# A new order of steps for a fused S5-scan and Hedgehog-attention kernel on one Trainium2 core

## The chip, the cores and the metric

The kernel runs on one core of one Trainium2 chip. The metric is the device time of one execution in microseconds (us), first instruction to last write. A core has a matrix engine (PE; its weight loads are listed apart as PEld), a vector engine (DVE), an activation engine (ACT), a general-purpose engine (POOL), and queues for DMA transfers, of which SP's is used most. Each engine works through its own list of instructions in order. Semaphores are the only tie between the lists.

## The reference

`x` has 2048 rows of 512. Two branches read it and a gate mixes them:

```python
x = A_x
g = _sigmoid((x * gate_w).sum(-1, keepdims=True))
a = _A_ref(x, ...)     # S5: h = Lam_bar * h + x @ B_bar over 2048 steps, y = 2 Re(h C) + x * Dskip
b = _B_ref(x, ...)     # q, k, v of 32 heads of 16; phi = [softmax(p), softmax(-p)]
return g * a + (1 - g) * b
...
# in _B_ref
kv = jnp.einsum("bhsf,bhsd->bhfd", phi_k, v)
num = jnp.einsum("bhqf,bhfd->bhqd", phi_q, kv)
den = jnp.einsum("bhqf,bhf->bhq", phi_q, z)[..., None] + 1e-6
o = num / den                                    # then o @ wo
```

## The kernel before

Rows are taken in 16 tiles of 128; row 8c + r is cell c of residue r. The scan is cut into eight residues, each step between residues being a matmul with a 128x128 block matrix of the powers of `Lam_bar` (`dg`), and a short scan over 64 groups of cells on DVE.

There is no loop nest to speak of. Every piece of work is a Python generator ("step") that issues a few instructions each time it is advanced. A table of some 1,300 tokens, `ORDER`, says in which order the generators are advanced; `k3@1` advances step `k3` and gives it PSUM bank 1, and `:D` puts that piece's copy or scaling on DVE instead of ACT. Since each engine runs its list in order, the table fixes the lists of all five engines:

```python
    for tok in ORDER.split():
        tok, _, banks = tok.partition("@")
        tok, _, eng = tok.partition(":")
        sel["eng"] = "dve" if eng == "D" else "act"
        sel["banks"] = [int(b) for b in banks]
        next(st[tok])
```

The PSUM banks are handed over by the same table: a step that is given bank 7 waits until the last reader of bank 7 is through.

The steps that matter here, by stage (`n` a tile, `m` one of eight blocks of states):

- **Start.** `Lk`, `Lx`, `Lv`, `Lb`, `Lc`, `Lq` load weights and `x` (transposing DMAs on SP's queue, L244 for `xT`); `Z` are matmuls on zeros that keep PE busy; `W`, `T`, `f` transpose and fold weights.
- **Small parameters.** `P`, `U`, `M` form `Lam_bar` and its powers on DVE in tiles of 128x8 (`dgs`; `M` has three parts, each squares the one before). `M2` carries on from the last of them on POOL: `M2`'s first part squares twice more (L419 to L421, twice), its second negates (L437), its third (L439 to L447, nine instructions) ends in two copies into `csp`, the scale factors of `C`. `dc` (L451, L452) stands on POOL between the second and the third.
- **Keys and queries.** `k`, `q`, `v` project a tile (L521) and copy it out of PSUM; for `q`, DVE also reads one column, `nge` (L555), and only then is the bank free. `x`, `n`, `e`, `s` (capital letters for queries) are the softmax pieces: maximum and minimum trees (L569), differences (L580, L587), exponentials on ACT (L594), sums and division. `a` adds up `kv`.
- **Scan.** `b` and `g` (L655, L660, L672 to L690) do the input products and the steps between residues; `z`, `sa`, `sb`, `H` the scan over groups and its corrections, which DVE adds into `HH` (L750).
- **C.** `c0` to `c3` scale the transposed `C` by `csp`, three parts each, into `CS` and `CT` (L470 on ACT, L472 on DVE); `C` and `A` move the results.
- **Fill-in of the other residues.** `hk`, `hd`, `ek`, `dk`: two scalings and two additions (L820, L822) per pair of blocks into `LS`.
- **Output.** `y` (L876, L883), `o` (L893; then L898, L901 on ACT and L907 on DVE), `O` (transposing DMA), `t` (L932, then a scaled copy out of PSUM), `R` the store.

The third part of `M2` ends so, and `c1`'s first part is the second line of `st_c`, with `j` = 1:

```python
        nc.gpsimd.tensor_copy(out=csp[0:HS], in_=dgb[0:HS, :, 0::2])
        nc.gpsimd.tensor_copy(out=csp[HS:P], in_=dgb[HS:P, :, 1::2])
...
    def st_c(j):
        scaled(CS[:, 1, j], CT[:, 0, j], csp[:, 1, j:j + 1])
```

Of the kernel before, what the change touches and what calls it, by code (L numbers as in the profile page):

```python
# [23 lines left out]
ORDER = """
Lk Z@0 Lk Z Z Z Z B Z B Z Z Z Z Z Lx Lx Z Z Z Z W00@2 Lx W01@1 W00 W01 W00 W01 W10@3 W11@4 W11:D f1@2 f0@1 T0@5 W10
f1 f0 T0:D Lx f2@4 V@3 T1@2 f3@6 Lx V f2 Z k0@5 P T1:D U P f3 k1@2 k1 Lv P2 P k0 P2 U k3@1 P2 k2@6 P2 k7@4 P2 P4 P3
P2 P3 P4 U Lx P4 i i M i Lb x0z U k5@0 k4@3 k1 M k3 k0 V2@1 i k7 i v0@4 n0 k5 x0 M k2 Lb v1@6 x0 n0 V2 k6@2 Lx v6@1
k4 i v3@3 k8@5 n0 x0 n0 x1 k9@0 n1 x0 Lx x1 L x0 n1 k10@7 n0 k6 v1 x2 M2 M2 Lx Lb x2 v6 e0 k11@2 x1 n1 x2 Lb k8 n1
x1 x2 x1 Da k13@5 v3 v0 Lq n2 k12@4 k15@3 k14@1 n1 dc n2 e1 s0 k9 k11 n2 x2 n2 b10@0 Da k15 k14 n2 Lc k10 s0 b10 k13
k12 g10@3 b00@2 M2 b31@5 b01@0 Lc s0 b21@4 x3 b20@7 e2 Lq Da s0 b11@1 e2 b00 x3 Db b30@6 g00@2 g10 b31 b21 w1@4 x3  # L30
g11@5 b01 Lc b20 g10 x4 s1 n3 g20@3 w1 w3@7 s1 s0 x4 b11 g20 gw g00 b30 Lc c1:D w2@6 c2 w3 g30@1 s1 g11 n3 w0@7 Da
s1 x3 g21@4 s0 g20 g31@3 Lb g00 g11 g21 s2 c0:D g30 c2 w0 g31 c2 s2 x4 g21 n3 Db x3 n4 w2 g21 n3 g11 g30 x4 g01@7
g21 g01 g11 s2 s1 g01 g21 g31 g11 g01 q3@1 g01 n4 g11 s2 g31 s1 g31 c3:D v4@6 c3 c1:D s0 n4 g31 g01 g31 g21 n3 q3 s2
x4 g31 g21 q0@2 g01 s2 Db s1 Lb g31 n4 g21 v4 q3 g11 q10@0 g01 g11 g21 q4@6 q0 e3 s2 v2@4 q0 n4 g11 g01 g31 c3:D g01
v5@1 q4 q2@3 z0@5 c0:D z0 q1@2 b61@7 z0 c1:D e3 q4 z0 s3 v2 a0@65 a0 q1 q10 b50@4 z0 s3 v5 q1 a1 q10 a1 a2 q7@1 s3
q2 a2 b40@0 e4 q7 N0 z0@2 q2 X0 g50@3 b61 a2 v7@7 z0 N0 X0 z0 X0 b50 q5@2 e4 C N0 v7 X0 b71@4 N0 q6@7 q7 c0 z0 X0 s3
q5 a2 s4 b40 A g50 N0 v9@1 q6 q5 X1 C q9@0 sa0@2 A b71 b60@4 g50 q6 v9 g40@1 X1 E0 N1 q9 C A g40 s4 b70@7 X1 b60 sa0
q8@2 X1 sb0@4 E0 s4 q9 N1 g70@3 b70 q8 X1 sb0 g40 s4 v8@0 g60@7 v8 s3 g70 s4 S0 H1@4 N1 S0 Lo g70 q8 g60 s3 G0 S0 N1
S0 v11@0 g71@2 b51@3 N1 g60 S0 g71 q11@1 H0@7 g71 S0 v11 g61@0 S0 C b51 s4 g61 H1 S0 v10@4 q11 g51@3 XX0 s3 a3 H0 E1
g71 v10 E1 g71 g71 g61 g51 b41@4 g51 g61 b41 XX0 A Ld a3 s4 a3 g61 g71 g51 g61 q11 a3 hd0 S1 X2 g41@1 g41 hd0 N2 g41  # L40
S0 g51 q13@4 g41 X2 g41 N2 X2 S1 g61 g71 g61:D g71 S0 G0 g51 XX0 S1 g51 g41 g41 v13@7 N2 g71 g51 S1 XX0 g51 hd0 g61
N2 X2 hd1 g41 g41 hd1 q12@2 g61 g41 g51 z1@1 v13 z1 z1 q14@0 v12@3 S1 hd0 q13 G0 z1 hd0 z1 z1@1 S1 hd1 v12 v15@7 z1
z1 q13 v14@1 z1 hd1 Ld X2 hd1 sa1@3 a4 v15 q15@4 sa1 v14 a4 N2 sb1@1 a4 sb1 END a4 Y hd0 Y q12 y0@3 H2@1 H3@7 S1 q14
Y E2 XX1 q14 Y H2 q15 y0 hk4 o3@5 o2@0 o2 H3 o3 o2 S1 XX1 q12 y3@7 y1@2 o3 y0 q15 E2 XX1 XX1 S1 o2 o0@0 o3 hd1 o0
o1@4 G1 y2@6 N3 y3 y2 o1 y1 y1 o0 hk6 o1 y3 S2 O1 hk4 o0 S2 o1 y2 O0 S1 N3 X3 hk6 o4@4 o5@0 hk6 hk4 hk6 o4 o4 hk4 S2
hk4 S2 t2 o4 hk6 o5 t2 hk4 S2 o5 t3 y4@5 t3 S2 y6@6 S2 ek0 o5 hk6 ek0 t0 X3 ek2 y5@7 S2 t0 y5 ek2 G1 O2 o7@3 X3 N3
ek2 X3 N3 ek0 o6@0 o6 y4 X3 o7 o6 t1 N3 o7 o6 S2 y5 S2 t5 ek0 o7 y7@0 ek0 y6 t1 y4 E3 o8@3 o9@1 ek2:D ek2 E3 ek0 ek4
o8 G1 y6 o8 y7 y7 ek2 ek4:D t4 o9 ek4 o9 ek6 O3 ek6:D ek6 t7 R1 t6 ek4:D ek6:D S3 o8 y9@3 y8@4 ek4 t6 o9 o10@1 ek4
t4 t5 t7 ek6 S3 y10@5 o10 ek6 o11@6 o10 XX2 XX2 y9 S3 y11@0 o11 y8 o10 O4 S3 R0 o11 y8 o11 S3 S3 y9 S3 y10 dk2 u10
S3 y11 dk0 S3 dk2:D t8 dk0:D dk0 dk0 dk2 R3 dk0 t9 dk2 O5 dk0 dk4 dk2 t10 dk4:D dk4 dk2 dk4:D y14@6 t8 dk4 t10 t11  # L50
t9 S3 dk6:D o12@4 o13@1 S3 dk6 o12 R4 y13@3 y12@7 o12 dk6:D o13 dk4 o13 o12 o14@4 o13 dk6 o14 R2 o14 dk6 dk6 y15@12
o14 y13 y12 o15@4 u11 y12 o15 y14 t11 o15 y14 y13 O6 t12 O7 R5 t13 t14 o15 O8 t12:D t13:D t14:D y15 R6 R7 y15 t15
t15 R8 t15 t15:D R8
"""
# [964 lines left out]
```

## Time and profile before

| | us |
|---|---|
| median of 3 executions | 146.94 (146.64 to 147.11) |
| the profiled execution, its whole time | 146.70 |
| its span, first to last instruction | 144.7 |
| PE, DVE, ACT, POOL busy in the span | 138.2, 132.9, 125.4, 21.9 |
| mean granted PE clock | 0.996 |

The profiled execution's time is 2.0 us above its span, and 0.24 us below the median. In the tables of the profile a row of the timeline gives start, length, engine, line of the kernel, operation, output and inputs, shape, and how many instructions were merged into it; lengths of neighbours overlap by some hundredths of a us to 0.17 us, since engines overlap the end of one instruction with the start of the next, so what an instruction adds to a full engine is the distance from its start to the next one's. PE has 986 matmuls and the trace holds records of 971 of them; a hole of exactly one matmul's length on PE is a missing record and no wait.

### The profile page before, as it was taken

The page shows a single profiled execution, that of the slowest core. Times are in us where ns is not written, and L with a number is a line of the kernel's source. Part 1 is how long each engine was busy: PE and PEld are TensorE (multiplying, and loading weights), DVE is VectorE, ACT ScalarE, POOL GpSimd, SP SyncE. Part 2 cuts the span into 40 slices and gives each one's busy share as a digit, 9 for nine tenths or more (in the row PEclk, how much of TensorE's full clock was granted, in tenths as well). Part 3 has the DMA queues.
Part 4 walks back from the last instruction along what each step waited for, and adds up shares of the span by engine and source line. Part 5 has one row for each costly group of instructions (what it writes and reads, how often), then busy time and mean ns, then how long its engine had stood idle before and what let it go on. Part 6 is the DMA issues. An engine that isn't in the chain of part 4 may idle for free.

```text
span 144.7 us, 2815 instructions
## 1 busy us (share of the span) xinstructions
PE 138.2 (96%) x971; PEld 74.9 (52%) x986; DVE 132.9 (92%) x313; ACT 125.4 (87%) x245; POOL 21.9 (15%) x40
## 2 busy tenths in 40 slices
PE   6999999999999999999999999999999999999990
...
DVE  5389999999999999999999999999999999999560
ACT  0899998999999999999999999999999996984110
...
GB/s 115 219 231 230 202 184 201 174 212 131 5 70 2 0 128 239 0 67 107 181 64 210 211 89 116 146 173 150 202 112 127 273 189 243 210 290 163 117 137 36
DMA packets 55957, 21.56 MB, mean 149 GB/s; under 512 B 44552, under 2 KB 55944, under 8 KB 55944
## 3 DMA queue, kind: packets, MB, share of 16 engines
...
q8 instruction: 7, 0.11, 0.4%
q14 instruction: 6, 0.05, 0.1%
...
## 4 chain that ended last, share of the span: by engine, by line
PE 79%; DMA 9%; SPq 4%; DVE 3%; issue 1%; ACT 1%; ACTq 0%
PE PS L521 20%; PE PS L876 17%; PE PS L660 10%; PE PS L655 10%; PE PS L932 9%; DMA xT<-in_A_x_dram 7%; PE PS L645 3%; SPq L244 3%; PE PS L893 2%; DMA CS<-in_B_wqkv_dram 2%; PE PS L672 2%; PE PS L883 2%; DVE HH L750 1%; PE PS L678 1%; SPq L249 1%
## 5 line engine op out<-in xcount | busy, mean ns | idle before, releaser
L594 ACT ACTIVATE EE<-EE 128x2048 bf16<-128x2048 bf16 x16 | 31.8, 2002 | 0.5 <-DVE EE L587 0.5
L521 PE MATMUL PS<-WKV,xT 128*128 128x480 bf16 (+1 forms) x124 | 28.8, 373 | 0.4 <-DMA xT<-in_A_x_dram 0.2
L521 PEld LDWEIGHTS <-xT 128*128 128x128 bf16 x192 | 18.3, 99 | 19.1 <-DMA xT<-in_A_x_dram 0.6
L876 PE MATMUL PS<-C,LS 128*128 128x512 bf16 (+1 forms) x102 | 22.7, 362 | 0.1
L141 ACT CAST Xq<-PS 128x480 bf16<-128x480 f32 x32 | 19.0, 640 | 0.2
L655 PE MATMUL PS<-xT,BT 128*128 128x512 bf16 x64 | 16.1, 379 | 0.0
L141 ACT CAST LS<-PS 128x512 bf16<-128x512 f32 x24 | 15.8, 735 | 0.1
L521 PE MATMUL PS<-Wq,xT 128*128 128x481 bf16 x64 | 15.6, 368 | 0.0
L660 PE MATMUL PS<-xT,BT 128*128 128x512 bf16 x64 | 15.5, 379 | 0.0
L932 PE MATMUL PS<-Wo,oT 128*128 128x512 bf16 (+2 forms) x64 | 14.8, 366 | 0.2
L569 DVE TENSOR_TENSOR EE<-EE 128x256 bf16<-128x256 bf16 (+3 forms) x54 | 14.6, 302 | 0.0
L876 PEld LDWEIGHTS <-LS 128*128 128x128 bf16 x104 | 9.3, 98 | 9.3 <-DVE LS L822 0.3
L938 ACT ACTIVATE ot<-PS,G 128x512 bf16<-128x512 f32 (+1 forms) x11 | 7.0, 671 | 5.4 <-PE PS L932 5.3
L907 DVE TENSOR_TENSOR on<-PS,rd 128x512 bf16<-128x512 f32 x16 | 10.6, 680 | 0.5 <-ACT rd L901 0.4
L470 ACT ACTIVATE CT<-HH,dgs 128x512 bf16<-128x512 bf16 x16 | 11.1, 722 | 0.0
L569 DVE TENSOR_TENSOR EE<-Xq 128x1024 bf16<-128x1024 bf16 (+1 forms) x18 | 11.0, 623 | 0.0
L141 ACT CAST vx<-PS 128x512 bf16<-128x512 f32 x16 | 10.9, 710 | 0.0
L470 ACT ACTIVATE CT<-CS,nsn 128x512 bf16<-128x512 bf16 x15 | 10.6, 726 | 0.0
L580 DVE TENSOR_TENSOR EE<-Xq,EE 128x2048 bf16<-128x2048 bf16 (+1 forms) x9 | 10.0, 1110 | 0.0
L587 DVE TENSOR_TENSOR EE<-EE,Xq 128x2048 bf16<-128x2048 bf16 (+1 forms) x9 | 9.9, 1105 | 0.0
L660 PEld LDWEIGHTS <-BT 128*128 128x128 bf16 x64 | 6.1, 98 | 6.9 <-issue 0.2
L932 PEld LDWEIGHTS <-oT 128*128 128x128 bf16 x68 | 6.2, 98 | 6.6 <-DMA oT<-on 0.7
...
## 6 DMA issues: line engine op xcount, KB each, us to landing
...
```

The lines of the kernel that those rows point to most:

```text
L141: nc.scalar.copy(out=out_ap, in_=in_ap)
L470: nc.scalar.mul(out=out_ap, in_=in_ap, mul=s_)
L521: MM(out=pt[:], lhsT=xT[:, kt, ti * P:(ti + 1) * P], rhs=W[:, kt, 0:pt.shape[-1]], start=(kt == 0), stop=(kt == KT - 1))
L569: VT(out=dst, in0=cur[:, :, :, 0:n, :], in1=cur[:, :, :, n:2 * n, :], op=op)
L580: VT(out=half(EE, 0), in0=X5, in1=live["mx", p].to_broadcast([P, L, 8, Dh, 4]), op=ALU.subtract)
L587: VT(out=t, in0=live["mn", p].to_broadcast([P, L, 8, Dh, 4]), in1=X5, op=ALU.subtract)
L594: aexp(out=EE[:, l_:l_ + w], in_=EE[:, l_:l_ + w], func=ACT.Exp)
L655: MM(out=pt[:], lhsT=BT[:, m, kt, :], rhs=cells(kt, r), start=(kt == 0), stop=False, skip_group_check=True)
L660: MM(out=pb[:], lhsT=BT[:, m, kt, :], rhs=cells(kt, 2 * pr), start=(kt == 0), stop=(kt == KT - 1))
L876: MM(out=py[:], lhsT=hs[m], rhs=C2[:, m, c:c + w], start=(m == 0), stop=False)
L907: VT(out=live["on", g_][:, u], in0=pn[:, :, :, 0:Dh], in1=rd[:].unsqueeze(3).to_broadcast([P, 2, 16, Dh]), op=ALU.mult)
L932: MM(out=py[:], lhsT=oT[:, g, :], rhs=Wo[:, g, c:c + w], start=False, stop=(g == HG - 1))
```

## The change

Only the table `ORDER` is different; every generator, buffer, shape and DMA is the same, and each token is still there as often as before. So the engines get the same work in another order, except that some of the `:D` marks moved: nine pieces go from DVE to ACT (`T0`, `c0`'s first part, one evacuation of `g61`, four scalings of `dk`, the copies of `t12` and `t14`) and seven from ACT to DVE (`f0`, `c3`'s second part, one scaling of `ek6`, four of `dk`). Banks are given out anew too.

```diff
 ORDER = """
...
-k4 i v3@3 k8@5 n0 x0 n0 x1 k9@0 n1 x0 Lx x1 L x0 n1 k10@7 n0 k6 v1 x2 M2 M2 Lx Lb x2 v6 e0 k11@2 x1 n1 x2 Lb k8 n1
-x1 x2 x1 Da k13@5 v3 v0 Lq n2 k12@4 k15@3 k14@1 n1 dc n2 e1 s0 k9 k11 n2 x2 n2 b10@0 Da k15 k14 n2 Lc k10 s0 b10 k13
-k12 g10@3 b00@2 M2 b31@5 b01@0 Lc s0 b21@4 x3 b20@7 e2 Lq Da s0 b11@1 e2 b00 x3 Db b30@6 g00@2 g10 b31 b21 w1@4 x3
...
+n1 k12@4 U k13@0 Lq M U k14@2 x2 s0 x1 s0 n1 s0 k8 k15@5 v1 x2 g00@6 M2 M2 k11 dc M2 x2 k10 n2 e1 b00@7 k13 Da b10@0
+k12 Lc k15 b11@1 b20@5 k14 n2 b21@4 v3 x3 c1:D s0 x4 n3 Lc Lq Db b00 Da Db e2 x3 e2 x4 b21 g11@7 g20@3 b30@2 s1 b20
...
```

Three places of the lists are used by the prediction, all on DVE. In an order row, `128x32x64` is the 128x2048 of the profile, `128x16x64` its 128x1024.

**The last squaring of `M` on DVE.** `ssm_par` and `dgs` are the tiles of the powers; POOL's `M2` waits for the row `L421` of the last of the three parts. Before, that part stands between the first trees of the keys:

```order
L569 TENSOR_TENSOR EE<-Xq 128x16x32 x2
L419 TENSOR_TENSOR ssm_par<-dgs 128x32
L420 TENSOR_TENSOR dgs<-ssm_par 128x8
L421 TENSOR_TENSOR dgs<-ssm_par 128x8
L569 TENSOR_TENSOR EE<-EE 128x16x16 x2
L356 CAST vecm<-PS 128x8
```

Now:

```order
L366 RECIPROCAL ssm_par<-ssm_par 128x8
L419 TENSOR_TENSOR ssm_par<-dgs 128x32
L420 TENSOR_TENSOR dgs<-ssm_par 128x8
L421 TENSOR_TENSOR dgs<-ssm_par 128x8
L368 TENSOR_SCALAR ssm_par<-ssm_par 128x8
L569 TENSOR_TENSOR EE<-EE 128x32x8
L569 TENSOR_TENSOR smk<-EE 128x1024
L580 TENSOR_TENSOR EE<-Xq,EE 128x16x64
L569 TENSOR_TENSOR smk<-smk 128x32x16
L587 TENSOR_TENSOR EE<-EE,Xq 128x16x64
```

It moved back, behind the first two groups of keys, to just ahead of the first row of sums, `smk<-EE`.

**The first use of `csp` on DVE**, `c1`'s first part (L472, `CS<-CT,csp`). Before:

```order
L569 TENSOR_TENSOR EE<-Xq 128x32x32
L569 TENSOR_TENSOR smk<-smk 128x32x16
L569 TENSOR_TENSOR EE<-EE 128x32x16
L415 CAST Wq_85<-vecm 128x4
L472 TENSOR_SCALAR CS<-CT,csp 128x512
L569 TENSOR_TENSOR smk<-smk 128x32x8
```

Now, a little further down the same list as the rows of the first place:

```order
L569 TENSOR_TENSOR smk<-smk 128x32x8
L569 TENSOR_TENSOR EE<-EE 128x32x4
L580 TENSOR_TENSOR EE<-Xq,EE 128x32x64
L569 TENSOR_TENSOR EE<-EE 128x32x4
L458 CAST dgv<-dgs 64x3x2x8x4
L460 CAST dgv<-dgs 64x24x4 x2
L587 TENSOR_TENSOR EE<-EE,Xq 128x32x64
L569 TENSOR_TENSOR EE<-Xq 128x32x32
L472 TENSOR_SCALAR CS<-CT,csp 128x512
L569 TENSOR_TENSOR smf<-smk 128x128
```

It moved forward, to two rows behind the first `L587 ... 128x32x64`; POOL's own list is the same but for one exchange ahead of `M2`.

**The hand-over from the scan to the output on DVE.** `L750 HH<-PS,HH 128x2x256` are the last additions of the scan, `L555 nge` frees a bank of a query, `L629` is a long product of the query features, `L907` an output tile. Before, with the second `L847` and what follows:

```order
L555 TENSOR_SCALAR nge<-PS 128x1
L847 SCALAR_TENSOR_TENSOR KVm<-PS,eps_p,maskN 128x16
L750 TENSOR_TENSOR HH<-PS,HH 128x2x256 x2
L629 TENSOR_TENSOR EE<-EE,rho 128x32x64
L555 TENSOR_SCALAR nge<-PS 128x1 x2
L907 TENSOR_TENSOR on<-PS,rd 128x512 x2
```

Now:

```order
L847 SCALAR_TENSOR_TENSOR KVm<-PS,eps_p,maskN 128x16
L750 TENSOR_TENSOR HH<-PS,HH 128x2x256 x2
L555 TENSOR_SCALAR nge<-PS 128x1 x2
L629 TENSOR_TENSOR EE<-EE,rho 128x32x64
L555 TENSOR_SCALAR nge<-PS 128x1
L907 TENSOR_TENSOR on<-PS,rd 128x512 x2
```

Two of the three `nge` reads stand ahead of the long `L629` now instead of one; with the new banks (`y1@5`, `y2@4`, `y3@2` in place of `y3@7`, `y1@2`, `y2@6`) the first two output tiles behind `o3` and `o2` take the banks that these two free.

More of the change, by code (lines that the diff above doesn't have):

```diff
@@ L24 @@
 ORDER = """
-Lk Z@0 Lk Z Z Z Z B Z B Z Z Z Z Z Lx Lx Z Z Z Z W00@2 Lx W01@1 W00 W01 W00 W01 W10@3 W11@4 W11:D f1@2 f0@1 T0@5 W10
-f1 f0 T0:D Lx f2@4 V@3 T1@2 f3@6 Lx V f2 Z k0@5 P T1:D U P f3 k1@2 k1 Lv P2 P k0 P2 U k3@1 P2 k2@6 P2 k7@4 P2 P4 P3
-P2 P3 P4 U Lx P4 i i M i Lb x0z U k5@0 k4@3 k1 M k3 k0 V2@1 i k7 i v0@4 n0 k5 x0 M k2 Lb v1@6 x0 n0 V2 k6@2 Lx v6@1
-k4 i v3@3 k8@5 n0 x0 n0 x1 k9@0 n1 x0 Lx x1 L x0 n1 k10@7 n0 k6 v1 x2 M2 M2 Lx Lb x2 v6 e0 k11@2 x1 n1 x2 Lb k8 n1
-x1 x2 x1 Da k13@5 v3 v0 Lq n2 k12@4 k15@3 k14@1 n1 dc n2 e1 s0 k9 k11 n2 x2 n2 b10@0 Da k15 k14 n2 Lc k10 s0 b10 k13
@@ L30 @@
-k12 g10@3 b00@2 M2 b31@5 b01@0 Lc s0 b21@4 x3 b20@7 e2 Lq Da s0 b11@1 e2 b00 x3 Db b30@6 g00@2 g10 b31 b21 w1@4 x3
[L31 to L53, printed above, removed]
+Lk Z@0 Z Z B Z Z Lk Lx Lx Z Lx Z Z Z Z Z Z Z Z Lx Z Lv W01@1 Z W00@2 W00 B W01 W00 W10@3 W11@4 Lx W01 f1@2 f0@1 T0@5
+V@0 W10 W11:D f0:D T1@3 Lb f3@6 f1 f2@4 V T1:D T0 P P P2 k0@5 f3 P2 Lx f2 P2 k1@2 k2@6 P2 P P2 k0 Lb P4 P4 k1 Lx
@@ new lines @@
+k3@1 P4 P3 P2 i k0 U i k1 i V2@4 n0 x0 P3 k4@3 i Lx k5@0 k6@2 n0 M k2 U k4 V2 k3 x0 k5 i x1 k6 x0 k7@4 n0 v6@1 x0
+v3@3 i n1 v1@6 M v0@2 k7 n1 n0 x1 L x0 n0 x2 k9@0 Lx v6 e0 x0z n2 k8@5 x1 Lb Lc n2 x2 n1 Lb n2 x1 k11@1 v0 k10@7 k9
+n1 k12@4 U k13@0 Lq M U k14@2 x2 s0 x1 s0 n1 s0 k8 k15@5 v1 x2 g00@6 M2 M2 k11 dc M2 x2 k10 n2 e1 b00@7 k13 Da b10@0
+k12 Lc k15 b11@1 b20@5 k14 n2 b21@4 v3 x3 c1:D s0 x4 n3 Lc Lq Db b00 Da Db e2 x3 e2 x4 b21 g11@7 g20@3 b30@2 s1 b20
+g00 x3 x4 g21@4 b10 g20 s1 c0 b30 b11 g10@0 n4 w3@1 s1 x3 c1:D n3 Lc g00 g20 g10 n4 s1 w0@6 b31@5 c2 g10 s0 s0 g11
@@ new lines @@
+n4 w0 g21 x4 g30@0 s2 b01@6 Da s2 g30 w2@3 b31 c2 gw c2 b01 g30 g11 Da g31@5 g11 x4 g31 g21 w3 n3 g21 w1@6 s2 g01@0
+s0 w1 c3:D s2 g01 s1 g01 g21 g11 w2 g31 q3@1 s2 Lb n4 g01 n3 x3 g21 g11 g01 s1 g31 g21 q3 v4@6 g01 g11 g21 g31 q0@2
+Db v4 c0:D n3 c3:D v2@6 g31 g11 g11 e3 s2 Lb q3 s1 g01 g01 g31 g21 g31 v5@1 c1:D q2@3 n4 g21 g01 g31 g11 c3:D q0
+b61@7 g01 g31 s2 q10@0 z0@5 q0 Ld z0 e3 b50@4 q10 q4@2 z0 s3 q2 v2 q10 q1@5 z0 a0@60 a0 v5 q4 s3 a1 a1 v7@1 z0 a2 q1
+e4 v7 s3 q4 q2 z0@2 q9@3 N0 q1 q5@5 e4 X0 a2 q7@1 z0 C b61 z0 a2 N0 q5 Ld z0 X0 s3 X0 v9@2 b50 N0 s4 q6@7 X0 b40@4
@@ new lines @@
+s4 a2 q9 v9 q7 q9 b70@3 q6 q5 Lo c0 v8@5 N0 g70@2 X0 q6 C N0 b70 s3 X1 N1 b40 E0 X1 C C g50@3 sa0@4 g50 A b71@7 q7
+s4 X1 g70 sa0 E0 g40@1 b71 X1 b60@4 g40 v8 b60 s4 g60@7 X1 S0 q8@4 sb0@5 N1 G0 S0 N1 g50 S0 v11@3 g70 sb0 A s3 g60
+g71@2 g71 H1@5 s4 A g40 v10@1 q8 g60 N1 S0 S0 b51@7 g71 N1 v11 S0 XX0 H1 s4 S0 E1 g51@3 b41@5 b51 g71 v10 g51 S0 A
+XX0 H0@7 s3 hd1 g51 g71 b41 g51 g71 g41@1 H0 a3 q11@7 g51 g41 E1 g41 g71 s4 g61@5 g51 g61 q11 g41 S1 g61 hd0 g71 g51
+g61 a3 g51 a3 hd0 q8 g41 a3 S1 q11 g61 g61 q13@4 G0 S1 g41 g61 X2 g71 g41 hd1 S0 hd0 g71 g51 N2 v13@7 g61 g61 g41
@@ new lines @@
+g41 S1 X2 g51 g41 XX0 S0 N2 q12@2 g61 hd1 q13 XX0 z1@1 q14@5 S1 v13 v12@3 X2 N2 z1 z1 N2 z1 G0 z1 q13 hd0 hd0 S1
+z1@1 v12 hd1 v15@7 q12 v14@3 z1 z1 v15 X2 z1 sa1@1 hd1 X2 a4 a4 q15@4 sa1 sb1@1 v14 a4 N2 a4 q15 sb1 XX1 XX1 y0@3 S1
+q14 Y H2@1 H3@7 Y y0 E2 Y y0 Y H2 H3 o3@0 hk4 END o2@6 XX1 q14 q15 y1@5 o3 S1 o2 XX1 o2 q12 o3 y2@4 o2 o0@6 S1 y3@2
+E2 o3 o1@0 hk6 hd0 o0 y3 y2 X3 y1 o1 hd1 y2 y3 o0 y1 S2 o0 o1 O1 o1 hk4 hk4 hk4 hk6 N3 S2 o5@0 hk6 o4@6 o4 O0 hk4 t2
+S2 o5 o4 hk4 S2 o4 ek0 S2 o5 N3 S1 S2 o5 t2 t3 y5@7 X3 y4@6 S2 hk6 t3 ek0 t0 t1 y7@0 S2 ek0 X3 o7@1 hk6 t0 N3 O2 t1
```

7 lines of the change are left out of this document (added).

## The prediction

> **What bounds the kernel now.** I read the page's shares and slices first, then DVE and PE in stretches, then POOL and DVE row by row where the lists change, then the waits of the tail.
>
> ```profile
> span 144.7 us, 2815 instructions
> PE 138.2 (96%) x971; PEld 74.9 (52%) x986; DVE 132.9 (92%) x313; ACT 125.4 (87%) x245; POOL 21.9 (15%) x40
> PE   6999999999999999999999999999999999999990
> DVE  5389999999999999999999999999999999999560
> ACT  0899998999999999999999999999999996984110
> ```
>
> Three engines are full at once until about 130 us. PE ends last, but DVE runs beside it without air:
>
> ```profile
> 27.50:80.00 52.50, 52.24 (x351) 27.29 (x355) 52.37 (x108) 52.27 (x97) 5.52 (x7) 1.00 0.59 102
> 80.00:90.00 10.00, 9.83 (x71) 5.29 (x69) 9.69 (x27) 9.70 (x28) 4.36 (x4) 1.00 0.71 141
> 90.00:133.00 43.00, 42.29 (x352) 23.24 (x357) 42.61 (x85) 39.79 (x82) 0.46 (x1) 1.00 0.92 188
> ```
>
> The columns are the stretch and the busy time of PE, PEld, DVE, ACT, POOL. From 27.5 to 133 us DVE idles 0.13 + 0.31 + 0.39 = 0.83 us in all. What ties it to PE at the end:
>
> ```profile
> 132.35 0.69 DVE L822 TENSOR_TENSOR LS<-CT 128x1024 bf16<-128x1024 bf16 x1
> PEld L876 <- DVE LS L822: 0.3, 1, 0.3
> ```
>
> The last addition of `dk6` ends at 133.04, and PE's weight load for the `y` that reads it waits 0.3 us; PE's margin there is some 0.07 us (the matmuls start at 133.11), and 7.8 us of PE work follow. So DVE's list up to this row is a second critical path, as long as PE's. PE cannot end earlier by more than this row does, and any delay on DVE from 27.5 us on that its 0.83 us of idle time doesn't take up comes out at the end.
>
> **The change, part by part.** *DVE's list up to `dk6`.* Ahead of that row six scalings (0.26 us each) and `f0` (0.34) came in, and five scalings, `T0` (0.41) and a small copy (0.14) went out: about +0.05 us, as an estimate from the rows' start-to-start times. So the order alone brings DVE there no sooner; only waits can differ.
>
> *A new wait: `c1` on POOL.* POOL's `M2` and `dc`, first and last rows and the third part in full:
>
> ```profile
> 15.49 0.24 POOL L419 TENSOR_TENSOR ssm_par<-dgs 128x32 f32<-128x32 f32 x1
> ...
> 17.67 0.69 POOL L437 TENSOR_SCALAR nsn<-dgs 128x16 f32<-128x16 f32 x1
> 22.31 0.11 POOL L452 MEMSET decay<- 128x8 f32 x1 [3.94 <-ACT decay L451]
> 22.38 0.46 POOL L439 TENSOR_TENSOR ssm_par<-dgs,vec 128x32 f32<-128x32 f32 x1
> 22.91 0.26 POOL L440 TENSOR_TENSOR dgb<-ssm_par 128x8 f32<-128x8 f32 x1
> 23.14 0.64 POOL L441 TENSOR_TENSOR dgb<-ssm_par 128x8 f32<-128x8 f32 x1
> 23.86 1.28 POOL L442 TENSOR_TENSOR dgb<-dgb,vec 128x16 f32<-128x16 f32 x1
> 25.22 0.69 POOL L443 TENSOR_TENSOR dgb<-dgb,ssm_par 128x16 f32<-128x16 f32 x1
> 26.02 1.41 POOL L444 TENSOR_SCALAR dgb<-dgb,sgn 128x8 f32<-128x8 f32 x1
> 27.39 0.34 POOL L445 TENSOR_SCALAR dgb<-dgb 128x8 f32<-128x8 f32 x1
> 27.80 0.50 POOL L446 COPY csp<-dgb 64x12 f32<-64x12 f32 x1
> 28.34 0.56 POOL L447 COPY csp<-dgb 64x12 f32<-64x12 f32 x1
> ```
>
> `csp` is ready at 28.90. DVE in the same stretch:
>
> ```profile
> 14.16 0.16 DVE L421 TENSOR_TENSOR dgs<-ssm_par 128x8 f32<-128x8 f32 x1
> ...
> 20.05 0.69 DVE L580 TENSOR_TENSOR EE<-Xq,EE 128x1024 bf16<-128x1024 bf16 x1
> 20.65 0.34 DVE L458 CAST dgv<-dgs 64x192 bf16<-64x192 f32 x1
> ...
> 22.04 0.68 DVE L587 TENSOR_TENSOR EE<-EE,Xq 128x1024 bf16<-128x1024 bf16 x1
> ...
> 23.04 0.68 DVE L569 TENSOR_TENSOR smk<-EE 128x1024 bf16<-128x1024 bf16 x1
> ...
> 23.86 1.21 DVE L580 TENSOR_TENSOR EE<-Xq,EE 128x2048 bf16<-128x2048 bf16 x1
> ...
> 25.15 0.68 DVE L463 TENSOR_TENSOR dg<-I,dgv 128x1024 bf16<-128x1024 bf16 x1
> 25.75 1.24 DVE L587 TENSOR_TENSOR EE<-EE,Xq 128x2048 bf16<-128x2048 bf16 x1
> ...
> 27.57 0.69 DVE L569 TENSOR_TENSOR EE<-Xq 128x1024 bf16<-128x1024 bf16 x1
> ...
> 32.61 0.35 DVE L472 TENSOR_SCALAR CS<-CT,csp 128x512 bf16<-128x512 bf16 x1
> ```
>
> Before, `c1` comes at 32.61, 3.7 us behind `csp`. Now it stands two rows behind the `L587` of 25.75, whose own place hardly moves: ahead of it `f0` and two rows of sums (0.34 + 0.41 + 0.21) came in, and `T0` and one `L463` (0.41 + 0.60) went out, so -0.05 us. 25.70 + 1.16 + 0.60 (start to next start of that row and of the 27.57 row) puts DVE before `c1` at 27.5.
>
> POOL starts later at the same time. The rows between the last squaring of `M` and that `L587` add up, start to start (0.60 for a 128x1024, 1.14 for the long L580, 0.78 for the casts at 20.65, the rest small trees), to 0.07 + 0.20 + 0.60 + 0.60 + 0.41 + 0.60 + 0.21 + 0.15 + 1.14 + 0.15 + 0.78 = 4.9 us, so `M` is through at 20.8 in place of 14.3, and `M2` cannot begin before. With the durations as they stand, 15.49 to 18.36 (2.87), `dc` 0.11 and 22.38 to 28.90 (6.52) give 20.8 + 9.5 = 30.3: a wait of 2.8 us. With all 17 at the shortest row of their kind (0.25, and 0.07 between them) it is 20.8 + 5.4 = 26.2 and no wait. Those are the bounds.
>
> Which end is nearer shows in the pairs. L441 ends at 23.78, DVE's `smk` at 23.72; L442 at 25.14, DVE's L580 at 25.07; L443 at 25.91, DVE's L463 at 25.83. A POOL instruction that meets a DVE one ends just behind it, whatever its own size. So I lay POOL's list beside DVE's new one: the six of the first part end with six DVE rows at 23.7; L437 meets the long L580 and ends at 24.9; `dc`, L439, L440 run beside the short casts to 25.7; L441 goes with the L587 to 27.0, L442 with the next row to 27.6. DVE then stands still, and the last five take 0.25 to 0.3 us each: 29.2. **The wait is 1.7 us.**
>
> The Trainium skill has a rule for these pairs ("SBUF — State Buffer", section "Who interferes with whom"): a DVE instruction with two inputs in SBUF holds the one read interface that GpSimd reads by, for its whole length, and the other side stands still. By that rule the long POOL rows are waits that end when DVE stops, which gives 1.7; by POOL's durations as its own it would be 2.8. The ends of the three pairs agree with the rule within 0.08 us.
>
> *What becomes of it.* Behind `c1` on DVE stand the building of `dg` for PE's `g`, the differences that ACT's exponentials wait for, and the `nge` reads that free banks, so PE and ACT fall back too. DVE's idle time of 0.83 us was waiting for those two, and part of it survives when they are late as well; I take half, 0.4. At `dk6`: 1.7 - 0.4 + 0.05 = 1.35, less PE's margin of 0.07: **+1.3 us**.
>
> *The hand-over at 93 us.* PE loses time there now:
>
> ```profile
> 93.92 1.02 PE L876 MATMUL PS<-C,HH 128*128 128x512 bf16 x4 [0.17 <-DVE HH L750]
> 95.13 1.02 PE L876 MATMUL PS<-C,HH 128*128 128x512 bf16 x4 [0.18 <-DVE nge L555]
> 93.80 1.20 DVE L629 TENSOR_TENSOR EE<-EE,rho 128x2048 bf16<-128x2048 bf16 x1
> 94.93 0.20 DVE L555 TENSOR_SCALAR nge<-PS 128x1 f32<-128x1 f32 x2
> 107.56 0.51 PE PS L893 x16
> ```
>
> Sixteen `o` matmuls take 0.51 us elsewhere and 0.83 here (93.09 to 93.92), four of `y` 1.21 (93.92 to 95.13) against 0.86. That is 0.67 us, and the new banks and the earlier `nge` rows remove nearly all. PE may gain it, but DVE does not, so at `dk6` it is lost again: 0 in the sum, -0.67 at best.
>
> *The start and the end.*
>
> ```profile
> 10.89 9.50 DMA xT<-in_A_x_dram
> 20.44 5.04 PE PS L521 x24
> ```
>
> PE waits at 20.44 for the fifth transposed load. The same seven transfers stand ahead of its landing in both lists, so an earlier or later start of PE by some tenths changes nothing: 0. The last tile and store keep their order: 0. `t12` and `t14` move from DVE to ACT, which idles there.
>
> Sum: 146.70 + 1.3 = 148.0 for an execution like the profiled one; the median lay 0.24 above it, so **148.2 us**.
>
> **Rivals.** *Faster:* POOL's short rows hold, `c1` finds `csp` ready, and DVE loses its waits where PE no longer delays it; then the hand-over counts, 146.94 - 0.67 = 146.3. For it: 0.83 us of idle time exist. Against: the POOL pairs. It decides the sign if `csp` comes before 27.9. *No change:* no wait at `c1`, but `dk6` stays where it is, with 0.07 us of margin; 146.9. *Larger:* POOL keeps its durations, 2.8 - 0.4: 149.4; for it speaks that none of its rows was seen with DVE silent, against it that the pairs end together.
>
> **How the numbers follow.** Forecast 0.58, larger 0.12, no change 0.12, faster 0.18. The forecast's own range, with 0 to 0.83 us taken up and a wait of 1.2 to 2.2 us, is 147.3 to 149.1; with the rivals 146.4 to 149.5. This kernel's executions spread such that 0.3% (0.44 us) is the least change that can be told. Slower 0.70, same 0.12, faster 0.18.
>
> **What would show it.** Right: DVE's L472 `CS<-CT,csp` first starts near 29.2 behind idle time of some 1.7 us put down to POOL `csp` L447; POOL's first L419 of `M2` starts near 20.8; the last DVE L822 starts near 133.7; PE's waits at 93 us are gone. Wrong: no idle time on DVE at 27.5 (then the rest of the sum is void), or a wait there of this size with `dk6` ending at 133.0 all the same, or PE losing time at another place that DVE does not cause.

## Result and the profile after

The changed kernel took **148.76 us** in the median of six runs (147.86 to 149.45), the kernel before 146.79 us beside it (146.45 to 147.73): a ratio of 1.012, with a 95% interval of 1.0071 to 1.0169. In the mean that is 1.8 us slower. Two of the six executions took 3.1 and 3.4 us more than their spans, the other four 2.0 to 2.1. The kernel before has such executions too (two in the round of w1, 3.1 and 3.4 us above their spans), but its figure there leaves them out as slow. So some 0.45 us of the 1.8 lie behind the last instruction, where no step of the order stands, and by spans the change costs about 1.3 us; whether the order has to do with those 0.45 us is not shown. The profiled execution took 148.51 us, its span is 146.5 us. First its page: the span, the engines, and the slices of PE and DVE.

```profile
span 146.5 us, 2815 instructions
...
PE 138.1 (94%) x970; PEld 74.7 (51%) x986; DVE 131.2 (90%) x311; ACT 126.2 (86%) x247; POOL 20.4 (14%) x40
...
PE   6999969999999999999999999999999999799990
...
DVE  5398999799999999999999999999999999988520
```

The work is the same as before (`ORDER` has 880 tokens in both kernels, not the 1,300 given above). The span is 1.8 us longer, and the slices show two holes in PE that were not there: the 6 in the sixth slice (18.3 to 22.0 us) and the 7 in the 35th (124.5 to 128.2 us). The windows, with the busy time of PE, PEld, DVE, ACT and POOL in each stretch:

```profile
20.40:27.50 7.10, 5.95 (x30) 2.85 (x31) 6.99 (x18) 6.43 (x12) 6.12 (x14) 1.00 0.87 189
27.50:80.00 52.50, 52.24 (x332) 26.88 (x336) 51.15 (x105) 52.27 (x97) 5.08 (x8) 1.00 0.56 106
...
90.00:133.00 43.00, 41.59 (x339) 22.61 (x343) 42.26 (x85) 39.14 (x80) 1.20 (x1) 1.00 0.94 191
```

PE's idle time lies in the first row (1.15 us) and the last (1.41 us), DVE's in the second (1.35 us, 0.13 before) and the last (0.74 us, 0.39 before). The waits of both engines by what released them (total us, times, longest):

```profile
PE PS L521 <- DMA xT<-in_A_x_dram: 1.4, 1, 1.4
...
DVE on L907 <- ACT rd L901: 0.9, 2, 0.6
...
PE PS L932 <- DMA oT<-on: 0.9, 1, 0.9
DVE CS L472 <- POOL csp L447: 0.9, 1, 0.9
...
DVE HH L750 <- PE PS L765: 0.3, 1, 0.3
```

Four places, then: DVE's forecast wait for `csp`; PE's wait for the fifth `xT` load; a new wait of PE's for `oT`; and, behind that, DVE's wait for `rd`. The first, on DVE:

```profile
25.76 1.23 DVE L587 TENSOR_TENSOR EE<-EE,Xq 128x2048 bf16<-128x2048 bf16 x1
26.90 0.71 DVE L569 TENSOR_TENSOR EE<-Xq 128x1024 bf16<-128x1024 bf16 x1
28.50 0.35 DVE L472 TENSOR_SCALAR CS<-CT,csp 128x512 bf16<-128x512 bf16 x1 [0.89 <-POOL csp L447]
```

and on POOL, the start of `M2` and the rows that end in `csp`:

```profile
20.80 0.29 POOL L419 TENSOR_TENSOR ssm_par<-dgs 128x32 f32<-128x32 f32 x1 [6.15 <-DVE ssm_par L368]
...
23.48 0.28 POOL L437 TENSOR_SCALAR nsn<-dgs 128x16 f32<-128x16 f32 x1
...
23.79 1.17 POOL L439 TENSOR_TENSOR ssm_par<-dgs,vec 128x32 f32<-128x32 f32 x1
...
25.78 1.29 POOL L443 TENSOR_TENSOR dgb<-dgb,ssm_par 128x16 f32<-128x16 f32 x1
27.17 0.62 POOL L444 TENSOR_SCALAR dgb<-dgb,sgn 128x8 f32<-128x8 f32 x1
27.77 0.22 POOL L445 TENSOR_SCALAR dgb<-dgb 128x8 f32<-128x8 f32 x1
28.05 0.19 POOL L446 COPY csp<-dgb 64x12 f32<-64x12 f32 x1
28.28 0.19 POOL L447 COPY csp<-dgb 64x12 f32<-64x12 f32 x1
```

`M2` starts at 20.80, DVE reaches `c1` at 27.61, `csp` is ready at 28.47, and DVE stands still for 0.89 us. The new wait shows in the chain of work that ended last (start, us, what), and on PE:

```profile
117.00 1.28 DVE on L907 x2
118.28 0.60 DVE CT L820
118.88 0.52 DVE Xq L569
119.39 7.29 DMA oT<-on
126.73 1.90 PE PS L932 x8
```
```profile
126.73 1.90 PE L932 MATMUL PS<-Wo,oT 128*128 128x512 bf16 x8 [0.90 <-DMA oT<-on]
```

PE is ready for `t8` at 125.8, and `O4`, the transposition that `t8` reads, lands at 126.69, 7.3 us after its issue. Before, `t8` followed at 125.00 without a wait:

```profile
123.70 1.46 PE L876 MATMUL PS<-C,LS 128*128 128x512 bf16 x6
125.00 2.75 PE L932 MATMUL PS<-Wo,oT 128*128 128x512 bf16 x12
```

The late PE makes `o12` and `rd` late, and DVE loses another 0.56 us ahead of `dk6`, whose last addition ends at 134.78 (133.04 before):

```profile
132.10 1.29 DVE L907 TENSOR_TENSOR on<-PS,rd 128x512 bf16<-128x512 f32 x2 [0.56 <-ACT rd L901]
133.31 0.68 DVE L820 TENSOR_TENSOR CT<-CT,LS 128x1024 bf16<-128x1024 bf16 x1
134.09 0.69 DVE L822 TENSOR_TENSOR LS<-CT 128x1024 bf16<-128x1024 bf16 x1
```

The hand-over at 93 us has got better, as forecast. The sixteen `o` matmuls take 0.68 us (94.12 to 94.80; 0.83 before, 0.51 undisturbed), and eight of `y` behind them run without a gap:

```profile
94.12 0.84 PE L893 MATMUL PS<-KVm,phT 128*128 128x68 bf16 x16
94.80 1.89 PE L876 MATMUL PS<-C,HH 128*128 128x512 bf16 x8
```

### The profile page after: what moved, and what is told of

The parts are those of the page before. It is cut to its first block, busy times and chain, and to the rows that moved or that the text cites. A ratio compares the mean times of both kernels' runs of the same rounds, so it can differ in the third digit from the quotient of the medians.

```text
span 146.5 us, 2815 instructions
## 1 busy us (share of the span) xinstructions
PE 138.1 (94%) x970; PEld 74.7 (51%) x986; DVE 131.2 (90%) x311; ACT 126.2 (86%) x247; POOL 20.4 (14%) x40
## 4 chain that ended last, share of the span: by engine, by line
PE 65%; DMA 15%; DVE 5%; SPq 5%; ACT 4%; issue 2%; ACTq 0%; DVEq 0%
PE PS L521 19%; PE PS L655 10%; PE PS L660 9%; PE PS L876 9%; DMA oT<-on 7%; DMA xT<-in_A_x_dram 6%; PE PS L932 5%; SPq L244 4%; PE PS L645 3%; DMA CS<-in_B_wqkv_dram 2%; PE PS L672 2%; PE PS L893 2%; ACT CT L470 2%; DVE on L907 2%; PE PS L883 1%
## 5 line engine op out<-in xcount | busy, mean ns | idle before, releaser
L594 ACT ACTIVATE EE<-EE 128x2048 bf16<-128x2048 bf16 x16 | 30.5, 1928 | 0.0
L141 ACT CAST Xq<-PS 128x480 bf16<-128x480 f32 x32 | 17.3, 591 | 0.8 <-PE PS L521 0.7
L569 DVE TENSOR_TENSOR EE<-EE 128x256 bf16<-128x256 bf16 (+3 forms) x54 | 14.1, 291 | 0.0
L141 ACT CAST LS<-PS 128x512 bf16<-128x512 f32 x24 | 13.7, 611 | 0.1
L470 ACT ACTIVATE CT<-CS,nsn 128x512 bf16<-128x512 bf16 x18 | 12.4, 719 | 0.0
L938 ACT ACTIVATE ot<-PS,G 128x512 bf16<-128x512 f32 (+1 forms) x13 | 8.4, 668 | 3.9 <-PE PS L932 3.9
L907 DVE TENSOR_TENSOR on<-PS,rd 128x512 bf16<-128x512 f32 x16 | 10.5, 681 | 0.9 <-ACT rd L901 0.9
L587 DVE TENSOR_TENSOR EE<-EE,Xq 128x2048 bf16<-128x2048 bf16 (+1 forms) x9 | 10.0, 1111 | 0.1
L580 DVE TENSOR_TENSOR EE<-Xq,EE 128x2048 bf16<-128x2048 bf16 (+1 forms) x9 | 9.9, 1100 | 0.0
L141 ACT CAST vx<-PS 128x512 bf16<-128x512 f32 x16 | 9.8, 620 | 0.0
```

The costliest lines, as they stand in the source:

```text
L141: nc.scalar.copy(out=out_ap, in_=in_ap)
L470: nc.scalar.mul(out=out_ap, in_=in_ap, mul=s_)
L569: VT(out=dst, in0=cur[:, :, :, 0:n, :], in1=cur[:, :, :, n:2 * n, :], op=op)
L580: VT(out=half(EE, 0), in0=X5, in1=live["mx", p].to_broadcast([P, L, 8, Dh, 4]), op=ALU.subtract)
L587: VT(out=t, in0=live["mn", p].to_broadcast([P, L, 8, Dh, 4]), in1=X5, op=ALU.subtract)
L594: aexp(out=EE[:, l_:l_ + w], in_=EE[:, l_:l_ + w], func=ACT.Exp)
```

## Experiments

The theories. **A**, the forecast: DVE's wait at `c1` is what comes out at the end. **B**: the fifth `xT` load, which landed at 21.50 us in place of 20.39, starts PE late, and that comes out. **C**: a share of the loss is made at PE's wait for `O4`. C can be so in two ways: **D**, `O4` is late because a packet that loads PE's instructions (queue 8) meets it on its way, and **E**, it is late because the two `CS<-LS` copies and the stores ahead of it on SP are. D needs two lines, one of the page of after, one of the view of its DMAs between 124.0 and 125.2 us:

```profile
q8 instruction: 7, 0.11, 0.3%
```
```profile
q8 instruction: 1, 0.02, 5.9%
```

In the span seven packets come on queue 8, 0.11 MB in all, 16 KB each. One of them takes 5.9% of 16 engines over 1.2 us, as much as one DMA engine for 1.1 us. In the records of single packets it lies at 124.04 to 125.17, just where the last end marks of `O4` are missing (a transposition's 256-byte packets are followed by 32 packets of 4 bytes, called marks here; presumably two come from each of the sixteen engines, but the records don't name the engine).

The hold-up reaches further than the two marks: from 124.64 to 125.94 us the changed kernel moves 35 packets of 256 bytes, and z2, a run below in which the packet lies elsewhere, moves 990 in the same stretch. `O5`, issued at 123.18, stands nearly still meanwhile.

### x1: the loads

```diff
 L267 DMA WKV<-in_B_wqkv_dram
-L244 DMA_TRANSPOSE xT<-in_A_x_dram
-L249 DMA C<-in_A_B_re_dram
-L244 DMA_TRANSPOSE xT<-in_A_x_dram
+L244 DMA_TRANSPOSE xT<-in_A_x_dram x2
+L249 DMA C<-in_A_B_re_dram
 L249 DMA C<-in_A_B_im_dram
```

> The changed kernel with one row moved on SP alone: the first plain load of C (in_A_B_re) goes behind the fourth transposed load of xT, so that both plain loads of C stand together, as before. Theory A (DVE's wait at c1 sets the end): the fifth transposed load lands near 20.4 us again in place of 21.5 and PE starts 1.1 us earlier, but DVE, which sets the end, only loses its two waits for PE (0.30 us at 71 us, 0.22 us at 86 us): 0 to 0.5 us faster than the changed kernel, ratio to before 1.009 to 1.012. Rival B (the late start of PE sets the end): 1.1 us faster, ratio 1.005. Landing still at 21.5: the order of the loads was not what made it late.

Measured: ratio 1.0126 (1.0088 to 1.0165). The fifth load still landed late, at 21.22. Six runs below with the changed kernel's own list of loads had it at 20.35, 20.58, 20.71, 21.42, 21.47 and 21.59, two runs with the list of before (y3, y4) at 20.50 and 21.44: the landing moves by 1.2 us from one execution to the next under the same list. So B is not borne out as a cause of the change, but a comparison of two profiles must allow for it.

### x2: c1 later

```diff
 L569 TENSOR_TENSOR EE<-Xq
-L472 TENSOR_SCALAR CS<-CT,csp
 L569 TENSOR_TENSOR smf<-smk
...
 L569 TENSOR_TENSOR EE<-EE x2
+L472 TENSOR_SCALAR CS<-CT,csp
 L569 TENSOR_TENSOR smk<-EE
```

> The changed kernel with the first scaling of c1 (L472, CS<-CT,csp) moved nine rows later on DVE, to about 31.9 us. Theory A: DVE's wait of 0.89 us for csp goes, csp itself comes at 28.5 to 29.4, and the end comes 0.5 to 0.9 us earlier: ratio to before 1.006 to 1.009. Rival B: DVE is late for PE's sake in any case, the wait's place is taken by others, 0 to 0.2 us, ratio 1.011 to 1.012.

Measured: ratio 1.0078 (1.0055 to 1.0101), 0.6 us better than the changed kernel, though the intervals overlap and the 0.45 us behind the last instruction stand on the changed kernel's side alone. DVE's wait for `csp` is gone. PE's wait at `t8` is still there, 0.92 us. POOL's last rows, now beside a busy DVE, are slower than in the changed kernel, and `csp` is ready only at 29.57:

```profile
27.45 0.74 POOL L444 TENSOR_SCALAR dgb<-dgb,sgn 128x8 f32<-128x8 f32 x1
28.16 0.62 POOL L445 TENSOR_SCALAR dgb<-dgb 128x8 f32<-128x8 f32 x1
28.84 0.50 POOL L446 COPY csp<-dgb 64x12 f32<-64x12 f32 x1
29.38 0.19 POOL L447 COPY csp<-dgb 64x12 f32<-64x12 f32 x1
```

L445 takes 0.62 us in place of 0.22, L446 0.50 in place of 0.19: the same rows, with DVE at work on two-input rows (28.01 to 29.29 us) and with DVE waiting. L447, beside a cast, keeps its 0.19. These rows agree with the rule of the Trainium skill that the prediction used ("SBUF — State Buffer", section "Who interferes with whom").

### x3: the transposition ahead of a store, and x4: all three

```diff
 L795 DMA CS<-LS x2
+L920 DMA_TRANSPOSE oT<-on
 L948 DMA out_dram<-ot
-L920 DMA_TRANSPOSE oT<-on x2
+L920 DMA_TRANSPOSE oT<-on
```

> The changed kernel with one row moved on SP alone: the fifth transposition of the outputs (oT<-on of 119.39 us) goes ahead of the store (out_dram<-ot of 118.85 us) that stands before it. Rival C (a share of the loss is made here): the transposition is issued near 118.3 and lands near 125.6, PE's wait of 1.0 us at 125.7 shrinks to below 0.3, DVE's wait of 0.56 us for rd at 131.5 goes, and the end comes 0.5 us earlier: ratio 1.008 to 1.009. Theory A alone: DVE's last LS addition was already late by 1.2 us, the end moves by 0 to 0.2 us.

Measured: ratio 1.0095 (1.0059 to 1.0131). `O4` was issued at 117.55, 1.8 us earlier, and nearly all its marks were written by 122.93 in place of 124.64; yet it landed at 126.34, and PE waited 1.3 us. That speaks against E: an earlier issue alone didn't help. The packet of queue 8 lay at 122.74 to 124.80 this time.

> The three edits of the runs x1, x2 and x3 together. If the loss of the changed kernel is made of these three: PE 1.1 + 1.0 us and DVE 0.89 + 0.56 us earlier than in the changed kernel, and the time is that of before within 0.4 us, ratio 0.997 to 1.003. If something else is in it too, it stays at 1.004 or above.

Measured: ratio 1.0086 (1.0056 to 1.0116). It stayed above 1.004, so the three edits do not take the cause away. No trace of it is read here.

### y1, y2, y3: the packet or the queue

y1 leaves out ten of the sixteen warm-up matmuls at PE's start, whose product nothing reads, and is otherwise x2; y3 does the same to the kernel before; y2 is x2 with two rows moved on SP.

```diff
 (y1, y3)
-L341 LDWEIGHTS Drow
-L341 MATMUL PS<-Drow
...
 (y2)
 L948 DMA out_dram<-ot
-L948 DMA out_dram<-ot
 L795 DMA CS<-LS x2
-L948 DMA out_dram<-ot
 L920 DMA_TRANSPOSE oT<-on
+L948 DMA out_dram<-ot x2
 L920 DMA_TRANSPOSE oT<-on
```

> The run x2 (first c1 scaling later) with ten of the sixteen warm-up matmuls of PE's start (L341) left out, 20 PE instructions less. In x2 PE's fourth wait was 1.08 us for the fifth oT transposition at 125 us; its packets and all but two of its 32 end marks were through at 123.98, the last two came at 125.27, and one 16 KB instruction packet (queue 8, one in about 250 PE instructions) held a DMA engine from 123.36 to 124.48. Theory D (that packet delays the transposition): it now comes about 1.1 us later, behind the transposition, PE's wait at 125 shrinks below 0.4 us, DVE's wait of 0.56 us for rd at 131.5 goes, and the time is that of before: ratio 1.000 to 1.004. Rival E (the transposition is late because the two CS<-LS copies and the stores ahead of it are late): the wait stays near 1.1 us, ratio 1.006 to 1.009. The six warm-up matmuls that are left end before the first load lands, so nothing else should move.

> The run x2 with SP's two stores (out_dram<-ot of 113.2 and of 118.2 us in x2) moved behind the fifth oT transposition, where they stood before. Rival E: the CS<-LS copies go out at once one behind the other again (0.6 us apart in place of 1.06), the transposition lands 1 us earlier and PE's wait at 125 us falls below 0.3 us: ratio 1.000 to 1.004. Theory D (the instruction packet): the transposition is through earlier too, but whether it escapes the packet hangs on tenths; a wait of 0.8 us or more there with all 256-byte packets through by 123.3 speaks for D: ratio 1.005 to 1.009.

> The kernel before with ten of its sixteen warm-up matmuls left out, nothing else: the control for y1. All theories: the same as before, ratio 0.998 to 1.002; PE's 16 KB instruction packet of 122.5 us comes at about 123.6.

Measured: y1 1.002 (0.9976 to 1.0064), y2 1.0000 (0.997 to 1.0031), and y3 **1.009** (1.0061 to 1.0119), where no theory expected a difference. In y1 and y2 PE's wait at `t8` is gone. In y3 it has appeared in the kernel before, at `t10`:

```profile
125.82 1.89 PE L932 MATMUL PS<-Wo,oT 128*128 128x512 bf16 x8
129.07 1.04 PE L932 MATMUL PS<-Wo,oT 128*128 128x512 bf16 x4 [1.36 <-DMA oT<-on]
```

Twenty PE instructions less had moved the packet from 122.51 to 126.45, into the next transposition, `O5`: 30 of its marks were written by 126.96, the last two at 128.31.

### y4: the forecast's wait alone, in the kernel before

```diff
 L569 TENSOR_TENSOR EE<-Xq
+L472 TENSOR_SCALAR CS<-CT,csp
 L463 TENSOR_TENSOR dg<-I,dgv
...
 L415 CAST Wq<-vecm
-L472 TENSOR_SCALAR CS<-CT,csp
```

> The kernel before with c1's first scaling (L472) moved from 32.61 to right behind the row of 27.57 on DVE, so that DVE waits there for csp (28.9) or for its part of CT: a wait of 0.7 to 1.2 us in a kernel that is otherwise before. Theory A: some 0.2 us of it are taken up by later idle time, the last LS addition comes 0.5 to 1.0 us later, and so does the end: ratio 1.0035 to 1.007; 1.01 or more if the fifth oT transposition runs into the instruction packet as well and PE waits there. Rival B: DVE has the air for it, below 1.002.

Measured: ratio 0.9995 (0.9956 to 1.0033). DVE waited, but only 0.49 us, and for its part of `CT`:

```profile
29.23 0.35 DVE L472 TENSOR_SCALAR CS<-CT,csp 128x512 bf16<-128x512 bf16 x1 [0.49 <-DMA CT<-in_A_C_re_dram]
```

It cost nothing that the interval could show. The price that A put on such a wait (one for one beyond 0.4 us) is not refuted by so small a wait, but nothing here supports it.

### z1, z2: each of the two alone

z1 is the changed kernel with y2's two rows moved, z2 the changed kernel without the ten warm-up matmuls; DVE's list is the changed kernel's in both.

> The changed kernel with SP's two stores moved back behind the fifth oT transposition and nothing else: DVE's wait at c1 stays. If the loss of the changed kernel is c1's wait plus PE's wait at 125 us, and the two add, this takes the second away: PE's wait for oT below 0.4 us, DVE's wait for csp still 0.8 to 0.9 us, the last LS addition near 134.0 to 134.3, ratio 1.003 to 1.006 (0.66 us of 147 is 1.0045). If c1's wait costs nothing by itself: 1.000 to 1.002. If the two do not add but the wait at c1 is what makes the transposition late: 1.010 or above.

> The changed kernel with ten of the sixteen warm-up matmuls of PE's start left out and nothing else: a second way to the same question, by moving PE's 16 KB instruction packet instead of the stores. The packet comes near 127 us, PE's wait for oT at 125 us falls below 0.4 us, DVE's wait for csp stays at 0.8 to 0.9 us; ratio 1.003 to 1.007. If another transposition meets the packet in its new place, PE waits there and the ratio is 1.010 or above.

Measured: z1 1.0045 (1.0018 to 1.0072), z2 1.0044 (1.0017 to 1.0072), from two different edits that have only the missing meeting of the packet and `O4` in common. DVE's wait for `csp` is 0.89 us in both, PE's wait at `t8` is gone. z2 decides between D and E: from 111.9 us to `O4`, SP's list and its times are those of the changed kernel within 0.1 us (`O4` issued 119.47, 119.39 in the changed kernel; its first 30 marks by 124.64 in both); what differs is the packet, which has moved to 126.62. On PE:

```profile
124.02 1.89 PE L876 MATMUL PS<-C,LS 128*128 128x512 bf16 x8
125.74 1.89 PE L932 MATMUL PS<-Wo,oT 128*128 128x512 bf16 x8
```

The marks, the packet and PE's wait, from the records of packets and PE's timelines (us):

| kernel | 30 marks by | last two marks | packet of queue 8 | PE waits |
|---|---|---|---|---|
| before, `O4` | 122.50 | 122.61 | 122.51 to 123.46 | 0 |
| changed, `O4` | 124.64 | **125.94** | 124.04 to 125.17 | 0.90 |
| x1, `O4` | 124.38 | **125.40** | 124.11 to 125.23 | 1.0 |
| x2, `O4` | 123.98 | **125.27** | 123.36 to 124.48 | 0.92 |
| z2, `O4` | 124.64 | 124.64 | 126.62 to 127.85 | 0 |
| y1, `O4` | 124.61 | 124.62 | 127.49 to 128.61 | 0 |
| z1, `O4` | 123.76 | 124.01 | 123.57 to 124.61 | 0 |
| y2, `O4` | 123.84 | 124.00 | 123.84 to 125.01 | 0 |
| y3, `O5` | 126.96 | **128.31** | 126.45 to 127.58 | 1.36 |

In the four rows in bold two marks are late, and they come behind the packet's end, by 0.2 us (x1) to 0.8 us (changed, x2). In before, z1 and y2 it begins 0.1 to 0.4 us ahead of the last mark and delays none: presumably its engine was through with its share, by tenths. (The marks of `O4` in x3 can't be told from those of its neighbours.)

In z2 and y1 the packet comes 2 to 3 us after the marks of `O4`, and there it meets another transposition, the `phT` that SP issued at 124.62 and 124.52. In y1 30 of its marks are written by 128.09 and the last two at 129.27; in z2 26 packets of 256 bytes move between 127.2 and 128.5 us, where the changed kernel moves 1473. PE's matmuls don't wait for it (in y1 a weight load does, 0.23 us): that `phT` lands at 129.90 (z2) and 130.07 us (y1), and PE's first weight load of it comes at 130.11 and 130.12. So leaving out the matmuls didn't free the kernel of a meeting. It moved the meeting to a transposition that PE needs later, and only just later enough.

The same executions from PE's first `g` matmul on (a start that moves from one execution to the next, with the `xT` load above all) to the last long L587 on DVE, and to the end of PE's last matmul:

| kernel | wait at `c1` | first `g` | to last L587 | to PE's end |
|---|---|---|---|---|
| before | no | 25.31 | 83.37 | 115.61 |
| y4 | 0.49 | 26.36 | 83.30 | 115.77 |
| changed | 0.89 | 26.42 | 83.00 | **116.24** |
| z1 | 0.89 | 26.39 | 83.02 | 115.60 |
| z2 | 0.89 | 26.50 | 82.99 | 115.57 |
| y2 | no | 26.33 | 83.00 | 115.57 |
| y1 | no | 26.19 | 83.20 | 115.78 |
| x2 | no | 25.26 | 83.49 | **116.75** |
| y3 | no | 26.18 | 83.31 | **117.09** |

Three things stand in it. The bold rows, with a meeting, are 0.6 to 1.5 us longer than their neighbours. The wait at `c1` doesn't show: with it (z1, z2) and without (y2) DVE and PE are in the same place. And 1.1 us of the 1.8 us between the two profiles is the later first `g` of that execution, behind an `xT` load whose landing moves as far without the change.

### z3 and w1: what is left in the order

z3 is y2 with both loads of `C` behind the fifth `xT` load; w1 is z3 with four warm-up matmuls less.

```diff
 L267 DMA WKV<-in_B_wqkv_dram
 L244 DMA_TRANSPOSE xT<-in_A_x_dram x3
-L249 DMA C<-in_A_B_re_dram
...
+L249 DMA C<-in_A_B_re_dram
+L249 DMA C<-in_A_B_im_dram
```

> The run y2 (first c1 scaling later, stores back) with the two plain loads of C moved behind the fifth transposed load of xT, to see whether the order with both repairs has something left in it: the fifth xT load lands 1 us or more earlier, PE's wait at 21 us goes, DVE's waits for PE at 71 and 86 us (0.30 and 0.22 us) go with it. Faster than before by up to 0.5 us, ratio 0.996 to 1.000; above 1.002 if BT, which is made from C, now comes too late for PE's b steps at 26 us.

> The run z3 (first c1 scaling later, stores back, plain loads of C behind the fifth xT load) with four of the sixteen warm-up matmuls of PE's start left out, 8 PE instructions less. In z3 PE still waited 0.87 us for oT at 125 us: the 16 KB instruction packet came at 123.56 us, between the end marks of that transposition (28 of 32 by 123.36). Eight instructions less should bring it 0.5 to 1 us later, behind the marks: PE's wait below 0.3 us, DVE's wait for rd at 131 us shorter by 0.3, and the end 0.3 to 0.5 us earlier than in z3: ratio 0.995 to 0.998, a version that beats both kernels. If the packet only meets the next transposition instead (needed at 128 us), PE waits there and the ratio is 0.999 or above.

Measured: z3 0.999 (0.9964 to 1.0016), with a meeting in its profile again (PE waits 0.71 us); that execution took 148.0 us, the median is 147.24, so the meeting may not stand in every execution of a kernel. w1 0.9987 (0.9949 to 1.0025), without one in its profile. Neither can be told from the kernel before, and both expectations were missed: in z3 PE still waited 0.84 us for an `xT` load, at 22.5 us. The changed order can be repaired, and no version was found that beats both.

## Why the prediction came out

The forecast was 148.2 us with a range of 146.4 to 149.5, and 148.76 was measured. The number held; most of its reason did not. That it held is luck: the wait was half as long as forecast and little or nothing of it came out, and the larger loss lies at a place that the forecast doesn't have.

**The ratios as a table.** Four cases, by whether DVE waits at `c1` and whether the packet makes PE wait for a transposition ("meeting"; x4, 1.0086, would stand beside x2 by its edits):

| | meeting | no meeting |
|---|---|---|
| wait at `c1` | 1.012, 1.0126, 1.0095 (changed, x1, x3) | 1.0045, 1.0044 (z1, z2) |
| no wait | 1.0078 (x2) | 1.0000, 1.002 (y2, y1) |

From row to row the wait is worth 0.0036 and 0.0034 in the mean, 0.5 us of 147. From column to column the meeting is worth 0.0069 and 0.0068, 1.0 us. Together that is 1.5 us; of the 1.8 us, some 0.45 lie behind the last instruction. The second is shown, by x2 against y2, whose intervals are apart, by z2's trace, and by y3 in the kernel before, in one round with it. The first is not firm: the intervals of z1 and y2 overlap, and no trace shows where it is paid. The median spans, each against the kernel before of its own round, give x1 1.4 us more and x3 1.1 (both), x2 1.1 (meeting alone), z1 0.5 and z2 0.7 (wait alone), y1 0.1 and y2 0.0 (neither), and y3 1.4. By these the wait adds 0 to 0.3 us to a meeting and 0.4 to 0.7 where there is none.

**1. DVE and PE both bound, DVE through `dk6`.** Right for the tail: from the end of `dk6` to PE's end it is 7.88 us before and after alike (133.04 to 140.92, 134.78 to 142.66), 7.87 or 7.88 in all fourteen profiles, and the hand-over's gain was given back there. In z1 and y2 PE comes from its first `g` to `t8` in 99.26 and 99.25 us, against 99.69 and 99.56 in before and y4; behind it they need 16.3 us, against 15.9 and 16.2. Wrong was "any delay on DVE from 27.5 us on that its 0.83 us of idle time doesn't take up comes out at the end". It holds only if PE isn't later still, and the `xT` load that PE starts behind moves by 1.2 us. y2 has no wait at `c1`, z1 has 0.89 us of it, and PE starts alike (26.33 and 26.39):

```profile
27.50:80.00 52.50, 52.50 (x338) 26.84 (x337) 51.48 (x105) 52.27 (x97) 5.95 (x8) 1.00 0.57 107
27.50:80.00 52.50, 52.50 (x337) 26.86 (x336) 51.26 (x105) 52.27 (x97) 5.15 (x8) 1.00 0.58 107
```

DVE (the third of the busy times; y2 first) idles 1.02 and 1.24 us there, up to 133 us 1.41 and 1.63, and `dk6` ends at 134.03 and 134.12: without the wait at `c1`, DVE waits for ACT and PE instead. The two earliest starts (25.3 us, before and x2) have no wait at `c1`, so what it costs beside such a start stays open. The profile of before, with its load at 20.39, was from the early end of that range, where DVE has the least air.

**2. The wait at `c1`.** Mechanism and place right: `M2` at 20.80 (forecast 20.8), DVE at `c1` at 27.61 (27.5), idle time put down to L447. The size is 0.89 us, not 1.7: I had laid POOL's L437 beside DVE's long L580, to end at 24.9, but it slipped in at 23.48, 0.15 us ahead of it (L439 met the L580 in its place, and L443 the L587), and only three rows, not five, were left when DVE stood still; they took 0.19 to 0.22 us, not 0.25 to 0.3. `csp` was ready at 28.47 instead of 29.2.

**3. The sum at `dk6`, +1.3 us.** This is the step that failed: the wait at `c1`, less 0.4 us, was to come out there. `dk6` ended 1.74 us later, 1.11 of it by the later first `g` of that execution. Counted from the first `g`, `dk6` ends at 107.73 us before, 107.73 in z1 and 107.70 in z2 (with the wait alone), and 108.36 in the changed kernel. So nothing of the wait shows in these traces, 0.5 us or so by the ratios; the larger part came from PE's wait for `O4` at 125.8 us, which the prediction has nowhere. It had named the sign itself ("PE losing time at another place that DVE does not cause"). DVE caused at most its occasion: the last scaling that reads `CS` ended 1.05 us later (115.95), about as much as the first `g` was later, and a store stands ahead of `O4` now; so `CS<-LS` and `O4` came later, into the packet. z2 shows that `O4` could be as late as it was without PE losing anything.

**4. The hand-over at 93 us.** Right: the loss there went from 0.67 us to 0.17 (16 `o` matmuls 0.68 us against 0.51), PE's way to `t8` is 0.3 to 0.4 us shorter, and nothing of it reaches the end.

**5. The start and the end at zero.** Not refuted. The list of loads makes no difference that x1 could show; the landing's own spread is larger than what was looked for.

Of the rivals, the larger one (149.4 us, POOL keeps its durations) is refuted by L445 and L446 (its sum, 146.94 + 2.4, gives 149.3); so are the faster one and "no change" in their reason, since the wait was there. The profile of before could have given the missing term only in part: the packet at 122.5 us and the transposition that ends there are in its DMA records, but which engine holds what when can't be told ahead to 0.1 us.
